# Operand blocks of a late batch prepared one by one, with the sums on VectorE and side work moved

## The chip, the cores and the metric

The kernel runs on one core of a Trainium2 chip. The metric is the device time of one launch in microseconds (us); of the kernel before, the median of three runs is 733.26 us (733.25 to 733.49).

## What is computed

Per batch and head, keys and values are pooled into 32 memory slots by a softmax over the slots, queries attend to those slots, and the result goes through a gated feed-forward layer. Cut to what matters:

```python
a = softmax(phi, axis=slots)                # 8 batches, 8 heads, 576 positions, 32 slots
k_m = einsum('bhsm,bhsd->bhmd', a, k)       # and v_m from v
attn = softmax(q @ k_m.T / 8)               # 576 x 32 per head
x = concat_heads(attn @ v_m)                # 4608 tokens x 512
out = (sigmoid(x @ w_gate) * (x @ w_val)) @ w_out     # 512 -> 1536 -> 512, float32
```

## The kernel before, in words

All engines run hand-written orders: `step` records an operation and chains it behind the last one of every engine it uses, so each engine executes exactly the order in which the program calls `step`.

Batches 0 to 3 and all loads come first (up to about 379 us); the change touches batches 4 to 7, the **late batches**, each some 87 to 89 us long. Such a batch has 12 steps f, one per 128 columns of the hidden layer (`for b, f`, from line 1312). Matrix products are made of three TensorE matmuls each, since every float32 operand is split into a rounded part `hi` (a ScalarE cast) and a rest `lo` (a VectorE subtraction, `rest`, line 179).

The transposed attention of a batch is a 2 x 2 block matrix, b11, b12, b21, b22, each 128 x 288. Seven products take the place of eight: `Group.p(1)` to `p(7)` multiply weight parts with b11, b21, b22 and four sums, t1 = b12 - b11, t2 = b22 - t1, t3 = t2 - b11, t4 = b21 - t2. Product to operand: 1 b11, 2 b21, 3 b22, 4 t4, 5 t1, 6 t2, 7 t3. b12 itself is no operand. Results land in PSUM banks a, b, c, d (one buffer each).

Order of a normal step (b, f), with h the group of the step before: p7 of h, p1, at even f the weights of the next two steps (`pair_u`, 16 small matmuls into banks c and a, copied out by ScalarE as `r_raw` and `l_raw`), one or two output products (`out_tile`: three 128 x 512 matmuls into an accumulator `acc`), p2 (into bank a), p5 (into c), perhaps one output product, p4 of h, p6, an output product, p3, an output product. VectorE adds and multiplies the results (`add`, `product_of`), ScalarE takes sigmoids (`gate`) and casts (`to_hi`, whose rest is `to_lo`); output products of step f run in step f + 2. `part_hi` and `part_lo` split the weights of the next pair, parts r, l and s.

Side work stands at named places of a step ("m", "act", "B", "m2", "end", "Z"), set by a plan per batch (`late_sides`, line 1255). While batch b runs, the plan prepares the attention of batch n = b + 1 (scores, softmax, `normalize`, `cross`, which transposes it into the tile of q, then `sums_at`) and the memory of batch m = b + 2. Loads of q, of the weight ring and the output stores go through SyncE's one queue.

The split operands live in four tiles `at` (128 x 1152 each: hi and lo of the blocks, hi and lo of the sums). There is no room for two batches, so at f = 11 the step **turns** (`turning`): p7 and p4 of the last group are made at once instead of in the next step, and `at_hi`, `at_lo` (lines 936 and 941) split the blocks and then the sums of the next batch, 1152 columns at a time, each behind the last product that reads the old tile. The next batch starts with no group h behind it. The four sums of batches 5 to 7 run on GpSimd (`sums_at(n, nc.gpsimd)`, lines 926 to 934).

Of the kernel before, what the change touches and what calls it, by code (L numbers as in the profile page):

```python
# [13 lines left out]
ALU = mybir.AluOpType  # L14
# [3 lines left out]
P = 128  # L18
B, H, S, D, M = 8, 8, 576, 64, 32
# [79 lines left out]
def attn_moe_kernel(  # L99
# [35 lines left out]
    def att(shape, name, bufs=1):  # L135
        return sb.tile(shape, F32, name=name, bufs=bufs)
# [214 lines left out]

    def a_exp(b):

        ph, nmx = loaded[b, "phi"], loaded.pop((b, "nmx"))
        z = loaded[b, "z"] = att([P, NG], "z")
        for g in range(NG):
# [568 lines left out]

    def sums_at(b, eng):

        (b11, b12, b21, b22), t = [
            [x[:, i * HALF : (i + 1) * HALF] for i in range(4)] for x in raw_at[b]
        ]  # L930
        eng.tensor_tensor(t[0], b12, b11, op=ALU.subtract)
        eng.tensor_tensor(t[1], b22, t[0], op=ALU.subtract)
        eng.tensor_tensor(t[2], t[1], b11, op=ALU.subtract)
        eng.tensor_tensor(t[3], b21, t[1], op=ALU.subtract)

    def at_hi(b, i):

        at.setdefault(b, {})[i] = [at_tile()]
        nc.scalar.copy(at[b][i][0].rearrange("p r n -> p (r n)"), raw_at[b][i])

    def at_lo(b, i):

        at[b][i].append(at_tile())
        hi, lo = [x.rearrange("p r n -> p (r n)") for x in at[b][i]]
        rest(lo, raw_at[b][i], hi)

    def attend(b):
        run(normalize(b))
        yield
        cross(b)  # L950
        sums_at(b, nc.vector)
        yield
# [146 lines left out]
    def side_of(b, name):  # L1099

        i, k = {"b11": (0, 0), "b21": (0, 2), "b22": (0, 3), "t1": (1, 0), "t2": (1, 1), "t3": (1, 2), "t4": (1, 3)}[name]
        return [x.rearrange("p r n -> p (r n)")[:, k * HALF : (k + 1) * HALF] for x in at[b][i]]

# [3 lines left out]
    class Group:  # L1107
# [133 lines left out]
    def out_tile():  # L1241

        if not tiles:
            return
        b, f, t, at_start, at_end = tiles.pop(0)
        hi, lo = [x[:, (t % 2) * P : (t % 2 + 1) * P] for x in G[b, f, t // 2]]
        w_hi, w_lo = wo_of(f)
        if at_start:
            acc[b, t] = po.tile([P, DM], F32, name=f"acc{t}")
        for i, (l, r) in enumerate([(hi, w_hi), (hi, w_lo), (lo, w_hi)]):  # L1250
            matmul(acc[b, t], l, r, start=at_start and i == 0, stop=at_end and i == 2)
        if at_end:
            leave(b, f, t)

    def late_sides(b):
# [11 lines left out]
        if n < B:  # L1267
# [10 lines left out]
            put(7, "act", s_exp, n)  # L1278
            put(8, "B", next, norm)
            put(9, "B", next, norm)  # L1280
            put(10, "B", cross, n)
            put(10, "Z", sums_at, n, nc.gpsimd)
        if m < B:
            def begin_m():
                memories[m] = memory(m)

            put(2, "B", a_max, m)
            put(7, "act", a_exp, m)
            put(7, "Z", a_sum, m)
            put(7, "Z", begin_m)  # L1290
            for f, place in ((8, "m2"), (9, "m"), (10, "m2"), (11, "m")):
                put(f, place, go, m)
                put(f, "end" if place == "m2" else "act", go, m)
            if m + 1 < B:
                put(11, "Z", load_next, m + 1)
        return plan

# [7 lines left out]
    for i in range(2):  # L1305
        step(at_hi, QUAD, i)
        step(at_lo, QUAD, i)
    raw_at.pop(QUAD)
# [3 lines left out]
    for b, f in [(b, f) for b in range(QUAD, B) for f in range(NFT)]:  # L1312
# [7 lines left out]
        n = (b - QUAD) * NP + f // 2  # L1320
        odd, turning = f % 2, f == NFT - 1
        more = n + 1 < NPAIRS
# [10 lines left out]
        if not late_left:  # L1333
            step(next, extra, None)
        wide = (b, f) in LEFT_AT and f != 5 or (f, "m") in plan or not odd and more
        if not odd and more:
# [3 lines left out]
        side("m")  # L1340
        side("m3")
        step(out_tile)
        if wide:
            step(out_tile)
        if h:
            step(h.product_of, 1)
        side("act")
        if not late_left:
# [21 lines left out]
        if h:  # L1370
            step(h.to_hi)
            step(h.to_left)
        if not odd and more:
            step(u_sums, n + 1, 0, 1)
# [5 lines left out]
        side("end")  # L1380
        if turning and b + 1 < B:
            step(at_hi, b + 1, 0)
        if not odd and more:
            step(part_hi, n + 1, "r")
        if odd and more:
            step(part_hi, n + 1, "s")
        step(g.add, 1)
        if late_left:
# [6 lines left out]
        if turning and b + 1 < B:  # L1395
            step(at_lo, b + 1, 0)
        step(g.gate, 0)
        step(g.gate, 1)
        if not odd and more:
            step(u_sums, n + 1, 2)  # L1400
            step(part_hi, n + 1, "l")
# [5 lines left out]
        if f == 0 and b + 1 < B:  # L1407
            load_q(b + 1)
        if h:
            for c in range(2):  # L1410
                put_tiles(h.b, h.f, c, h.f == 0, h.f == NFT - 1)
        if f == 0 and n:
            pairs_of.pop(n - 1)
        if not odd and f:
            pairs_of.pop(n - 1)
        h = g
        if turning:
# [13 lines left out]
            step(out_tile)  # L1431
            h = None
    extra = out_left(B // 2 - 1, 2 * TURN, TURN)
    step(next, extra)
    while tiles:
        step(out_tile)
    step(next, extra)

# [52 lines left out]
```

## Time and profile before

| what | value |
| --- | --- |
| median of three runs | 733.26 us |
| the profiled execution, its own time | 733.32 us |
| its span, first to last instruction | 731.5 us |
| PE busy, share of span | 713.2 us, 97% |
| VectorE (DVE) | 536.3 us, 73% |
| ScalarE (ACT) | 421.0 us, 58% |
| GpSimd (POOL) | 47.5 us, 6% |
| granted TensorE clock, mean | 1.00 |

A busy PE is one with a matmul in it. Since the starts of matmuls of one kind follow at a fixed distance when nothing is late, time lost is read from the distance of two starts. Idle time of the other engines costs nothing by itself.

### The profile page before, as it was taken

The numbers are of one execution on the slowest core, as the hardware profiler recorded it, in microseconds if no ns is written. First come the engines' busy times: TensorE is split into PE (matmuls) and PEld (weight loads), VectorE is DVE, ScalarE is ACT, GpSimd is POOL, SyncE is SP. The second block draws the span as 40 slices with busy tenths as digits, with TensorE's granted clock in tenths as the row PEclk, the third lists the DMA queues.
The fourth block names the chain that finished last, engine by engine and source line by source line (L and its number), as shares of the span: only waits on it lengthen the run. The fifth ranks groups of instructions, "written<-read, shape, count | busy, mean of one in ns | idle before, by whom it ended". The sixth has DMA issues, their size and how long they took to land.

```text
span 731.5 us, 14167 instructions
## 1 busy us (share of the span) xinstructions
PE 713.2 (97%) x5524; PEld 582.4 (80%) x5524; DVE 536.3 (73%) x1021; ACT 421.0 (58%) x969; POOL 47.5 (6%) x83
## 2 busy tenths in 40 slices
PE   8899999999999999999999999999999999999997
PEld 6656778888988988887987788778887887778786
DVE  5999998676877765577458678776787777977663
ACT  4676775464444433245366576765867557676553
POOL 0000100220111110110100002000020000200000
PEclk9999999999999999999999999999999999999999
DMA  8994629659348469861565222643114312141102
GB/s 347 418 386 159 239 87 389 206 162 369 133 159 288 146 194 234 286 225 29 171 274 184 63 110 92 231 150 110 66 59 163 133 58 73 58 173 59 58 1 72
DMA packets 37906, 124.64 MB, mean 170 GB/s; under 512 B 4240, under 2 KB 11664, under 8 KB 31696
## 3 DMA queue, kind: packets, MB, share of 16 engines
q1 hardware_dynamic: 31744, 103.04, 40.1%
q0 software_dynamic: 6096, 20.71, 7.9%
q8 instruction: 43, 0.70, 0.4%
q14 instruction: 23, 0.19, 0.1%
HBM read 94.90 MB, written 28.84 MB: 169 GB/s over the span
## 4 chain that ended last, share of the span: by engine, by line
PE 82%; DVE 11%; ACT 3%; DMA 2%; issue 1%; SPq 0%; DVEq 0%; ACTq 0%
PE acc L189 33%; PE pu_t L189 25%; PE c L189 8%; PE a L189 7%; PE d L189 4%; PE b L189 4%; DMA kvm<-in_kvm_dram 2%; DVE zs L495 1%; DVE at L179 1%; DVE z L1143 1%; DVE z L1150 1%; DVE e L482 1%; DVE e L499 1%; DVE mx L480 1%; DVE e L473 1%
## 5 line engine op out<-in xcount | busy, mean ns | idle before, releaser
L189 PE MATMUL pu_t<-at,u_hi 128*128 128x320 f32 (+1 forms) x752 | 156.2, 303 | 0.2 <-DVE sg L670 0.2
L189 PE MATMUL acc<-wo_hi,g_hi 128*128 128x512 f32 x372 | 151.1, 406 | 0.0
L189 PE MATMUL acc<-wo_hi,g_lo 128*128 128x512 f32 x372 | 147.2, 396 | 1.4 <-DVE g_lo L179 1.4
L189 PE MATMUL acc<-wo_lo,g_hi 128*128 128x512 f32 x372 | 146.5, 394 | 0.0
L189 PEld LDWEIGHTS pu_t<-at,u_hi 128*128 128x128 f32 x752 | 124.2, 188 | 11.8 <-issue 3.0
L189 PE MATMUL pu_t<-at,u_lo 128*128 128x320 f32 (+1 forms) x360 | 106.2, 295 | 0.0
L189 PEld LDWEIGHTS acc<-wo_hi,g_hi 128*128 128x128 f32 x372 | 69.8, 188 | 34.4 <-issue 14.2
L189 PEld LDWEIGHTS acc<-wo_hi,g_lo 128*128 128x128 f32 x372 | 69.8, 188 | 20.1 <-DVE g_lo L179 4.1
L164 ACT ACTIVATE sg<-pu_t 128x256 f32<-128x256 f32 (+1 forms) x94 | 38.7, 411 | 73.2 <-PE pu_t L189 73.0
L189 PEld LDWEIGHTS acc<-wo_lo,g_hi 128*128 128x128 f32 x372 | 70.0, 188 | 6.4
L670 DVE TENSOR_TENSOR sg<-pu_t,sg 128x256 f32<-128x256 f32 (+1 forms) x92 | 41.5, 454 | 39.9 <-ACT sg L164 27.3
L680 ACT CAST g_hi<-sg 128x256 fp32r<-128x256 f32 x90 | 36.4, 406 | 55.8 <-DVE sg L670 54.6
L189 PEld LDWEIGHTS pu_t<-at,u_lo 128*128 128x128 f32 x360 | 67.8, 188 | 0.0
L1139 ACT COPY c_p<-c 128x288 f32<-128x288 f32 x48 | 19.2, 400 | 56.7 <-PE c L189 56.7
L1155 ACT CAST g_hi<-z 128x512 fp32r<-128x512 f32 x48 | 29.8, 621 | 29.7 <-DVE z L1150 29.7
L179 DVE TENSOR_TENSOR g_lo<-sg,g_hi 128x256 fp32r<-128x256 f32 x90 | 37.4, 419 | 11.0 <-ACT g_hi L680 11.0
L1143 DVE TENSOR_TENSOR z<-c,c_x 128x288 f32<-128x288 f32 x48 | 21.8, 454 | 31.3 <-PE c L189 24.6
L1143 DVE TENSOR_TENSOR z<-a,c_s 128x288 f32<-128x288 f32 x48 | 21.9, 456 | 30.2 <-PE a L189 28.9
L164 ACT ACTIVATE z<-z 128x288 f32<-128x288 f32 x96 | 38.2, 438 | 8.5 <-DVE z L1143 8.2
L179 DVE TENSOR_TENSOR u_lo<-pu_t,u_hi 128x512 fp32r<-128x512 f32 (+1 forms) x46 | 28.6, 672 | 10.4 <-ACT u_hi L593 10.4
L179 DVE TENSOR_TENSOR g_lo<-z,g_hi 128x512 fp32r<-128x512 f32 x48 | 33.5, 698 | 3.7 <-ACT g_hi L1155 3.7
L593 ACT CAST u_hi<-pu_t 128x512 fp32r<-128x512 f32 (+1 forms) x46 | 24.0, 587 | 13.8 <-PE pu_t L189 13.7
(252 smaller groups left out, 1480.7 us busy)
## 6 DMA issues: line engine op xcount, KB each, us to landing
ring<-wgv SPq DMA_DIRECT2D x24, 1024.0 KB, 4.8
at<-at SPq DMA_DIRECT2D x24, 576.0 KB, 7.6
kvm<-in_kvm_dram SPq DMA_DIRECT2D x12, 1024.0 KB, 10.1
q<-in_qT_dram SPq DMA_DIRECT2D x16, 512.0 KB, 4.8
part<-row POOLq DMA_DIRECT2D x32, 256.0 KB, 4.8
row<-part SPq DMA_DIRECT2D x32, 256.0 KB, 4.0
wg<-in_kvm_dram SPq DMA_DIRECT2D x4, 1024.0 KB, 11.9
out_dram<-row POOLq DMA_DIRECT2D x16, 256.0 KB, 4.7
```

Of the source, the lines that this page charges most:

```text
L164: last_act[0] = nc.scalar.activation(*args, **kw)
L179: return nc.vector.tensor_tensor(lo, x, hi.bitcast(F32), op=ALU.subtract)
L189: last_pe[0] = do(*args, **kw)
L473: nc.vector.transpose(blocks(b, c)[:, r].rearrange("p w m -> p (w m)"), t)
L480: nc.vector.tensor_reduce(mx, e, axis=AX.X, op=ALU.max)
L482: nc.vector.tensor_tensor(e, e, mx.unsqueeze(3).broadcast_to([P, 2, w, M]), op=ALU.subtract)
L593: nc.scalar.copy(hi[:, r, :nf], U[b, fs[0], "pb"][r])
L670: last_prod[0] = nc.vector.tensor_tensor(prod, ps[1][:, :n], sg[:, :n], op=ALU.mult)
L680: nc.scalar.copy(hi, prod[:, : 2 * P])
L1139: nc.scalar.copy(getattr(self, name), self.c if name == "p5" else self.d)
L1143: nc.vector.tensor_tensor(self.z[:, i], x, y, op=ALU.add)
L1155: nc.scalar.copy(self.g[0], self.z[:, 2:4, : 2 * P])
```

## The change

1. The four `at` tiles become eight **rooms** of 288 columns (hi and lo). Seven hold the operands of the running batch, one is spare. When the last product that reads a room has been issued (f = 11, or f = 0 of the next batch for products 7 and 4), its room goes to the next free block of the next batch. `at_hi` and `at_lo` handle one block, in the order b11 (f = 10), b21, t1, t2 (f = 11), b22, t3, t4 (f = 0 of the next batch).
2. The turn goes: p7 and p4 of the last group run in the next batch's step 0, as in any other step, except in the very last step.
3. The four sums run on VectorE, two at f = 10 and two at f = 11.
4. Side work moves: `normalize` from places B of f = 8 and 9 to E and Z of f = 8, `cross` from f = 10 to the end of f = 9; the exponentials of `a_exp` are set apart; the cast of part l moves from the end of an even step to the start of the odd one, behind its first copy; the copies of the memory move with it; the copies of finished accumulators (`leave`) wait for `leave_late`; the load of the next batch's q stands behind the split of t4.

```diff
-    def at_hi(b, i):
...
-        at.setdefault(b, {})[i] = [at_tile()]
-        nc.scalar.copy(at[b][i][0].rearrange("p r n -> p (r n)"), raw_at[b][i])
...
+    def at_hi(b, name):
+        k = room_of_at[b, name] = free_rooms.pop(0)
+        nc.scalar.copy(at_rooms[k][0], raw_of(b, name))
+
+    def at_lo(b, name):
+        hi, lo = at_rooms[room_of_at[b, name]]
+        rest(lo, raw_of(b, name), hi)
...
             self.product(getattr(self, where), x, t, start)
+            if self.f == NFT - 1:
+                free_rooms.append(room_of_at.pop((self.b, t)))
...
-            put(8, "B", next, norm)
-            put(9, "B", next, norm)
-            put(10, "B", cross, n)
-            put(10, "Z", sums_at, n, nc.gpsimd)
+            put(8, "E", next, norm)
+            put(8, "Z", next, norm)
+            put(9, "Z", cross, n)
+            put(10, "B", sums_at, n, 1, 2)
+            put(10, "act2", at_hi, n, "b11")
+            put(10, "Z", at_lo, n, "b11")
+            put(11, "m", at_hi, n, "b21")
+            put(11, "E", sums_at, n, 3, 4)
+            put(11, "B", at_lo, n, "b21")
+            put(11, "act2", at_hi, n, "t1")
+            put(11, "B2", at_lo, n, "t1")
+            put(11, "act3", at_hi, n, "t2")
+            put(11, "Z", at_lo, n, "t2")
+        if b > QUAD:
+            put(0, "act", at_hi, b, "b22")
+            put(0, "act", at_hi, b, "t3")
+            put(0, "E", at_lo, b, "b22")
+            put(0, "B", at_lo, b, "t3")
+            put(0, "act2", at_hi, b, "t4")
+            put(0, "B2", at_lo, b, "t4")
...
-            put(7, "act", a_exp, m)
+            put(7, "act1", a_exp, m, (0,))
+            put(7, "act2", a_exp, m, (1,))
...
-                put(f, "end" if place == "m2" else "act", go, m)
+                put(f, "end" if place == "m2" else "m", go, m)
...
         side("m3")
+        if odd and more:
+            step(part_hi, n + 1, "l")
         step(out_tile)
...
-        if turning and b + 1 < B:
-            step(at_hi, b + 1, 0)
...
-        if turning:
+        last = b == B - 1 and f == NFT - 1
+        if last:
             step(g.p, 7)
             step(g.add, 3)
...
-        if f > 1:
+        if f > 1 or b > QUAD:
             step(out_tile)
...
-            if b + 1 < B:
-                step(at_hi, b + 1, 1)
-                step(at_lo, b + 1, 1)
-                raw_at.pop(b + 1)
...
-            h = None
```

Three places show how the engines' orders move (names: `at` split operands, `q` the raw blocks, `z` the group's results, `g_hi`/`g_lo` their split, `c_s`, `c_p`, `c_x` copies of banks, `r_raw`, `l_raw`, `s_raw` raw weights, `u_`/`s_` their splits).

ScalarE from step 11 of batch 6 into step 0 of batch 7, before and then with the change:

```order
L939 CAST at<-q 128x1152
L1085 CAST s_hi<-s_raw 128x768
L164 ACTIVATE z<-z 128x288 x2
L939 CAST at<-q 128x1152
L1155 CAST g_hi<-z 128x512
L1165 COPY left<-z 128x64
L1139 COPY c_s_7628<-d 128x288
L1067 COPY r_raw<-a 128x512
```

```order
L1171 CAST g_hi<-z 128x512
L1181 COPY left<-z 128x64
L957 CAST at<-q 128x288
L1101 CAST s_hi<-s_raw 128x768
L164 ACTIVATE z<-z 128x288 x2
L957 CAST at<-q 128x288
L1155 COPY c_s_7620<-d 128x288
L1083 COPY r_raw<-a 128x512
L1083 COPY l_raw<-c 128x512
L957 CAST at<-q 128x288 x2
```

The second cast of the last group (`g_hi`, `left`) no longer stands between the casts of `at` and the copy `r_raw`; two casts of 288 columns do, and more follow behind `l_raw`.

VectorE in step 10 of batch 6, from the results of step 9 to the rest `g_lo`, before and then with the change:

```order
L1143 TENSOR_TENSOR z<-b,c_p_7396 128x288
L1150 TENSOR_TENSOR z<-z 128x288
L1143 TENSOR_TENSOR z<-a,c_s_7456 128x288
L924 STREAM_TRANSPOSE q<-e 128x1152
L1150 TENSOR_TENSOR z<-b,z 128x288
L1082 TENSOR_TENSOR s_raw<-r_raw,l_raw 128x256
L1082 TENSOR_TENSOR s_raw<-s_raw,l_raw 128x256
L1143 TENSOR_TENSOR z<-c,c_x 128x288
L179 TENSOR_TENSOR g_lo<-z,g_hi 128x512
```

```order
L926 STREAM_TRANSPOSE q<-e 128x1152
L1159 TENSOR_TENSOR z<-b,c_p_7408 128x288
L1166 TENSOR_TENSOR z<-z 128x288
L1159 TENSOR_TENSOR z<-a,c_s_7470 128x288
L932 TENSOR_TENSOR q<-q 128x288 x2
L1166 TENSOR_TENSOR z<-b,z 128x288
L1098 TENSOR_TENSOR s_raw<-r_raw,l_raw 128x256
L1098 TENSOR_TENSOR s_raw<-s_raw,l_raw 128x256
L1159 TENSOR_TENSOR z<-c,c_x 128x288
L179 TENSOR_TENSOR g_lo<-z,g_hi 128x512
```

The transpose (`cross`) goes ahead of the step's three first operations, and two of the four sums (L932) come in where it stood.

ScalarE in steps 8 and 9 of batch 4, before and then with the change (`row<-a` copies the transposed weights of the memory out of bank a):

```order
L388 COPY row<-a 128x512
L1085 CAST u_hi<-r_raw 128x512
L164 ACTIVATE z<-z 128x288 x2
L1085 CAST u_hi<-l_raw 128x512
L1139 COPY c_s_5323<-b 128x288
L388 COPY row<-a 128x512
```

```order
L390 COPY row<-a 128x512
L1101 CAST u_hi<-r_raw 128x512
L164 ACTIVATE z<-z 128x288 x2
L1155 COPY c_s_5323<-b 128x288
L390 COPY row<-a 128x512
L1101 CAST u_hi<-l_raw 128x512
```

The cast of part l now stands behind the second copy out of bank a instead of ahead of it.

## Rows read from the trace of the kernel before

**Rows 1.** Batch 5: its length; busy PE, PEld, DVE, ACT, POOL; PE clock; DMA
```profile
468.62:557.60 88.98, 87.40 (x673) 70.53 (x674) 67.97 (x130) 60.11 (x138) 3.76 (x4) 1.00 0.29 100
```

**Rows 2.** Waits of PE, 380 to 732 us: for whom, us in total, times, longest
```profile
PE a L189 <- ACT r_raw L1067: 3.5, 3, 1.3
PE acc L189 <- DVE g_lo L179: 1.4, 2, 1.1
PE a L189 <- ACT row L388: 0.9, 2, 0.4
```

**Rows 3.** Timeline of PE at the turn from batch 4 to 5: start, us, what
```profile
462.25 0.39 PE L189 MATMUL acc<-wo_hi,g_hi 128*128 128x512 f32 x1
462.48 0.40 PE L189 MATMUL acc<-wo_lo,g_hi 128*128 128x512 f32 x1
462.90 0.50 PE L189 MATMUL acc<-wo_hi,g_lo 128*128 128x512 f32 x1
463.24 0.43 PE L189 MATMUL b<-at,u_hi 128*128 128x288 f32 x2
...
463.64 0.39 PE L189 MATMUL acc<-wo_hi,g_hi 128*128 128x512 f32 x1
...
464.83 0.61 PE L189 MATMUL c<-ring,vT 64*32 64x512 f32 x1
...
465.85 0.50 PE L189 MATMUL acc<-wo_hi,g_hi 128*128 128x512 f32 x1
...
467.12 0.39 PE L189 MATMUL acc<-wo_hi,g_lo 128*128 128x512 f32 x1
468.62 0.53 PE L189 MATMUL a<-at,s_hi 128*128 128x288 f32 x2 [1.12 <-ACT r_raw L1067]
```

**Rows 4.** Timeline of ScalarE at the same turn
```profile
463.75 1.16 ACT L939 CAST at<-q 128x1152 fp32r<-128x1152 f32 x1
467.02 0.62 ACT L1155 CAST g_hi<-z 128x512 fp32r<-128x512 f32 x1 [2.12 <-DVE z L1150]
...
467.69 0.39 ACT L1139 COPY c_s<-d 128x288 f32<-128x288 f32 x1
467.98 0.59 ACT L1067 COPY r_raw<-a 128x512 f32<-128x512 f32 x1
```

**Rows 5.** Timeline of VectorE at the same turn
```profile
465.27 1.35 DVE L179 TENSOR_TENSOR at<-q,at 128x1152 fp32r<-128x1152 f32 x1
466.54 0.45 DVE L1150 TENSOR_TENSOR z<-b,z 128x288 f32<-128x288 f32 x1
467.67 0.69 DVE L179 TENSOR_TENSOR g_lo<-z,g_hi 128x512 fp32r<-128x512 f32 x1 [0.69 <-ACT g_hi L1155]
```

**Rows 6.** Timeline of ScalarE, steps 8 and 9 of batch 4
```profile
441.92 0.61 ACT L1085 CAST u_hi<-l_raw 128x512 fp32r<-128x512 f32 x1
...
442.72 0.59 ACT L388 COPY row<-a 128x512 f32<-128x512 f32 x1
```

**Rows 7.** Timeline of VectorE, step 10 of batch 6
```profile
628.05 1.37 DVE L924 STREAM_TRANSPOSE q<-e 128x1152 f32<-128x1152 f32 x1
...
629.68 1.04 DVE L1082 TENSOR_TENSOR s_raw<-r_raw,l_raw 128x256 f32<-128x256 f32 x1
...
631.97 0.91 DVE L179 TENSOR_TENSOR g_lo<-z,g_hi 128x512 fp32r<-128x512 f32 x1
```

**Rows 8.** Timeline of PE, start of step 11 of batch 6
```profile
631.41 0.40 PE L189 MATMUL acc<-wo_lo,g_hi 128*128 128x512 f32 x1
632.94 0.50 PE L189 MATMUL acc<-wo_hi,g_lo 128*128 128x512 f32 x1 [1.14 <-DVE g_lo L179]
```

**Rows 9.** The first of the four sums: ns min/median/max, first and last start us
```profile
L931 POOL TENSOR_TENSOR q<-q x3: 804/809/811, 452.9 to 629.6; 128x288 f32<-128x288 f32 x3
L931 DVE TENSOR_TENSOR q<-q x1: 459/459/459, 337.1 to 337.1; 128x288 f32<-128x288 f32 x1
```

**Rows 10.** DMA issues of the page: KB each, median us from issue to landing
```profile
q<-in_qT_dram SPq DMA_DIRECT2D x16, 512.0 KB, 4.8
```

More of the change, by code (lines that the diff above doesn't have):

```diff
@@ L350, in a_max, with a_exp @@
         loaded[b, "nmx"] = nmx
[L352 to L356, printed above, removed]
+    def a_exp(b, gs=range(NG)):
+        ph, nmx = loaded[b, "phi"], loaded[b, "nmx"]
+        if 0 in gs:
+            loaded[b, "z"] = att([P, NG], "z")
+        z = loaded[b, "z"]
+        for g in gs:
             curve(
@@ L924, in cross, with sums_at, raw_of, first_hi @@
         nc.vector.transpose(raw_at[b][0], loaded[b, "e"])
[L926 to L934, printed above, removed]
-    def at_hi(b, i):
-        at.setdefault(b, {})[i] = [at_tile()]
-        nc.scalar.copy(at[b][i][0].rearrange("p r n -> p (r n)"), raw_at[b][i])
[L941 to L945, printed above, removed]
+    def sums_at(b, *which):
+        for i in which:
+            x, y = [("b12", "b11"), ("b22", "t1"), ("t2", "b11"), ("b21", "t2")][i - 1]
+            nc.vector.tensor_tensor(raw_of(b, f"t{i}"), raw_of(b, x), raw_of(b, y), op=ALU.subtract)
+    ROOMS = {"b11": 0, "b12": 1, "b21": 2, "b22": 3, "t1": 4, "t2": 5, "t3": 6, "t4": 7}
+    at_rooms, free_rooms, room_of_at = [], [], {}
+    def raw_of(b, name):
+        i, k = divmod(ROOMS[name], 4)
+        return raw_at[b][i][:, k * HALF : (k + 1) * HALF]
+    def first_hi(b, i):
+        if i == 0:
+            whole = [[at_tile() for _ in range(2)] for _ in range(2)]
+            whole = [[x.rearrange("p r n -> p (r n)") for x in part] for part in whole]
+            at_rooms.extend([x[:, k * HALF : (k + 1) * HALF] for x in part] for part in whole for k in range(4))
+            room_of_at.update({(b, name): k for name, k in ROOMS.items() if name != "b12"})
+            free_rooms.append(ROOMS["b12"])
+            at[b] = whole
+        nc.scalar.copy(at[b][i][0], raw_at[b][i])
+    def first_lo(b, i):
+        rest(at[b][i][1], raw_at[b][i], at[b][i][0])
+    def at_hi(b, name):
[4 more added lines that the diff above has]
+        rest(lo, raw_of(b, name), hi)
     def attend(b):
@@ L950, in attend @@
         cross(b)
-        sums_at(b, nc.vector)
+        sums_at(b, 1, 2, 3, 4)
         yield
@@ L1099, in side_of @@
     def side_of(b, name):
-        i, k = {"b11": (0, 0), "b21": (0, 2), "b22": (0, 3), "t1": (1, 0), "t2": (1, 1), "t3": (1, 2), "t4": (1, 3)}[name]
-        return [x.rearrange("p r n -> p (r n)")[:, k * HALF : (k + 1) * HALF] for x in at[b][i]]
+        return at_rooms[room_of_at[b, name]]
     def late_bank(name):
@@ L1252, in out_tile, with leave_late @@
         if at_end:
-            leave(b, f, t)
+            leaving.append((b, f, t))
+    leaving = []
+    def leave_late():
+        while leaving:
+            leave(*leaving.pop(0))
     def late_sides(b):
@@ L1292, in late_sides @@
                 put(f, place, go, m)
-                put(f, "end" if place == "m2" else "act", go, m)
+                put(f, "end" if place == "m2" else "m", go, m)
             if m + 1 < B:
                 put(11, "Z", load_next, m + 1)
+        if b + 1 < B:
+            put(0, "load", load_q, b + 1)
         return plan
@@ L1305, in attn_moe_kernel @@
     for i in range(2):
-        step(at_hi, QUAD, i)
-        step(at_lo, QUAD, i)
+        step(first_hi, QUAD, i)
+        step(first_lo, QUAD, i)
     raw_at.pop(QUAD)
@@ L1320, in attn_moe_kernel @@
         n = (b - QUAD) * NP + f // 2
-        odd, turning = f % 2, f == NFT - 1
+        odd = f % 2
         more = n + 1 < NPAIRS
@@ L1334, in attn_moe_kernel @@
             step(next, extra, None)
-        wide = (b, f) in LEFT_AT and f != 5 or (f, "m") in plan or not odd and more
+        wide = (b, f) in LEFT_AT and f != 5 or (f, "m") in plan and (f != NFT - 1 or b + 2 < B) or not odd and more
         if not odd and more:
@@ L1346, in attn_moe_kernel @@
             step(h.product_of, 1)
+        step(leave_late)
         side("act")
@@ L1353, in attn_moe_kernel @@
             step(part_lo, n + 1, "r")
+        side("E")
         step(g.add, 0)
         step(g.copy, "p5")
+        side("act1")
         if odd and more:
@@ L1372, in attn_moe_kernel @@
             step(h.to_left)
+        side("act2")
         if not odd and more:
@@ L1387, in attn_moe_kernel @@
         step(g.add, 1)
+        step(leave_late)
         if late_left:
             step(next, extra, None)
-        if turning:
+        last = b == B - 1 and f == NFT - 1
+        if last:
             step(g.p, 7)
@@ L1394, in attn_moe_kernel @@
             step(h.to_lo)
-        if turning and b + 1 < B:
-            step(at_lo, b + 1, 0)
+        side("B2")
         step(g.gate, 0)
         step(g.gate, 1)
+        side("act3")
         if not odd and more:
             step(u_sums, n + 1, 2)
-            step(part_hi, n + 1, "l")
         if odd and more:
             step(part_lo, n + 1, "s")
-        if f > 1:
+        if f > 1 or b > QUAD:
             step(out_tile)
         side("Z")
-        if f == 0 and b + 1 < B:
-            load_q(b + 1)
+        side("load")
         if h:
@@ L1411, in attn_moe_kernel @@
                 put_tiles(h.b, h.f, c, h.f == 0, h.f == NFT - 1)
[L1412 to L1415, printed above, removed]
+        if (f == 0 or not odd) and n:
+            pairs_of.pop(n - 1, None)
         h = g
-        if turning:
+        if last:
             step(out_tile)
@@ L1436, in attn_moe_kernel @@
         step(out_tile)
+        step(leave_late)
     step(next, extra)
```

## The prediction

> **What bounds the kernel now.** First the busy time by stretch: in batch 5 PE has a matmul in it for 87.40 of 88.98 us, DVE for 67.97, ACT for 60.11 [rows 1]. PE sets the time; a gain must come out of the 1.58 us in which it stands still, and work moved between DVE, ACT and POOL counts only where PE waits for it. [...] Next the waits of PE over the late batches: three for `r_raw`, 3.5 us in all, two for `g_lo`, 1.4, two for the memory's copy `row`, 0.9 [rows 2]. Last the timelines, to see what each stall costs and what stood ahead of its releaser.
>
> **A stall costs more than its idle time.** Matmuls of an output product start 0.23 us apart (462.25, 462.48). At the turn the third starts 0.42 after the second: 0.19 lost, though no idle time is listed. The next start then comes 0.34 later instead of 0.23, 0.11 more to refill [rows 3]. Later PE starts its last output matmul at 467.12 and the next product at 468.62: 1.50 instead of 0.23, 1.27 lost for 1.12 listed [rows 3]. So I add 0.15 and a refill of 0.11 to each listed wait.
>
> **Why PE waits at the turn.** Product 2 of the new batch needs bank a, which holds raw weights until ACT's copy `r_raw` at 467.98, 0.59 long, has ended, at 468.57 [rows 4]; PE had filled the bank soon after its last weight matmuls, so before 465.85 [rows 3]. ACT came late because it first waited 2.12 us for the old group's result, cast it (`g_hi`, 467.02) and copied `c_s` [rows 4]. That result (DVE, 466.54) stood behind the second split of `at`, 1.35 long from 465.27 [rows 5]. So the chain is: split of 1152 columns, result, cast, copy, PE.
>
> **Removed.**
> - The three `r_raw` waits: 3.5 + 3 x (0.15 + 0.11) = 4.3.
> - The short `g_lo` stall ahead of each turn, where products 7 and the added `add` crowd in: 3 x (0.19 + 0.11) = 0.9, taking the other two turns for like the first.
> - The `row` waits at step 9 (batches 4 and 5): 0.9 + 2 x 0.26 = 1.4. Product 2 waits there for the copy of 442.72; ahead of it stands the cast of part l, start 441.92, 0.61 long [rows 6]. The cast goes behind the copy, which takes more off than the 0.45 that each of the two waits lists, so they end. Who then waits for the later cast: `part_lo` l, on DVE, behind the first result of step 9; its product is in step 10, so nobody on PE.
> - The `g_lo` waits of batch 6: 1.4 + 2 x 0.26 = 1.9. The large one is 632.94 after 631.41, 1.53 instead of 0.23 [rows 8]. On DVE `cross` (1.37) stood in step 10 ahead of the chain to `g_lo`, and the weight sums behind it took 1.04, `g_lo` 0.91 against 0.69 at the turn [rows 5, 7] while POOL made its sums from 629.6 on [rows 9]. Now `cross` is at the end of step 9 and POOL is still. The small one, at step 9, stood behind `normalize`; it moves into the idle time of DVE ahead of the first result of step 8.
>
> Sum of what can go: 4.3 + 0.9 + 1.4 + 1.9 = 8.5.
>
> **Added.** Per turn DVE gets four sums of 0.46 [rows 9], 1.84. The early batches ran one there at that price. Eight splits of 288 columns take the place of two of 1152. No row has them: DVE's nearest is the 288-column result, 0.45 [rows 5], so 3.6 against 2.7; bounds 0.34 (a quarter of 1.35) and 0.69 (512 columns) [rows 5]. I take 0.45, the same size and engine. On ACT eight casts at 0.39, by the copy of the same size [rows 4] (bounds 0.29, a quarter of 1.16, and 0.61 [rows 6]), 3.1 against 2.3. DVE gains about 2.7 busy us, ACT 0.8; DVE gets back what POOL's sums cost it, 0.6 for one weight sum alone if it takes the 0.4 of a 288-column operation. In batch 5 that makes DVE about 70 of 89, so it does not bound a batch; the question is the three steps at a turn.
>
> **The turn counted through.** I took the new orders of the four engines from step 8 to step 1, each operation behind its engine's last and behind what it reads, with the durations above, 0.08 of overlap between neighbours (465.27 to 466.54 is 1.27 for an operation of 1.35 [rows 5]), products at 0.40 (463.24 to 463.64) and output products at 0.70 [rows 3]. Steps 10 and 0 last 6.7 us on PE (seven products, four output products, 1.0 for raw weights, 464.83 to 465.85 [rows 3]), step 11 lasts 5.6, in batches 4 and 5 some 2.3 more for memory matmuls. The tightest turn is 6 to 7, without them. There, from product 7 of step 11 on: DVE works on step 11's list from 1.2 to 8.3, that is 2.7 us into step 0; `product_of(0)` of group 10 is done at 5.1, before product 1 of the new step, which writes its bank, at 6.0. ACT follows it: cast 5.6, t1, part s, two sigmoids, t2, `c_s`, then `r_raw`, done at about 8.7. Product 2 can start at 8.9. The blocks are ready in time: b11 at 1.2 for 6.0, b21 at 4.7 for 8.9, t1 at 6.8 for 9.3, t2 at 8.3 for 10.1, b22 at 10.0 for 11.2, t3 at 10.7 for 12.3, t4 at 13.3 for 15.3. At the other two turns everything has 1 to 2 us more. Step 10 of batch 6 ends `g_lo` 0.8 before its need. So I expect no stall of size; I allow 0.4 for the 0.2 of room at the tightest place.
>
> **Moved past queues.** The q load on SP now waits for the split of t4 (about 13.3, near the end of step 0), with only output stores and weight-ring loads behind it. Its first use is step 3, some 18 us from the start of step 0; two loads of 4.8 us [rows 10] and a smaller one end before it even one after the other. Later accumulator copies on ACT free `acc` one step ahead of reuse. GpSimd's queue only loses work. PE keeps all its matmuls. Cost zero; were q late by 5 us, scores would stall PE for that in two batches.
>
> The sum, against the profiled execution of 733.3 (span 731.5; it is 0.06 from the median): 733.3 - 8.5 + 0.4 = **725.2 us**.
>
> **The rivals.**
> - *The wait survives at the turn.* ACT still casts t1 and t2 and part s ahead of `r_raw`, behind the result of group 10, which DVE gives only after sums, splits and weight rests. If DVE is a microsecond later than I count, product 2 waits as before. If each turn keeps 1.3 us, 3.9 comes back: 729.1. For: room of 0.2 at turn 6 to 7. Against: 1 to 2 us at the others.
> - *Slower: DVE bounds the turn.* Over steps 10, 11 and 0 DVE has at full durations 15 results (6.8), five rests of 512 columns (3.5), one of 768 (about 1.0) and six weight sums (some 0.4 each, 2.4), 13.7 us, and 5.4 of splits and sums: 19.1, against 19.0 for PE at the last turn. If no overlap holds and each block waits for ACT's cast and delays the results behind it, PE waits for lo parts and bank releases one after another. It decides from 3.3 us of new wait per turn (9.9 against 8.5); at 3.5 the time is 735.3. Against: the 0.08 overlaps and the 21 us at the other turns. [...]
> - *No change:* the stall shifts to another wait at the turn and the other gains are eaten: about 733.
>
> **How the numbers follow.** The forecast, 723.8 to 727.3, has 0.60; the surviving wait, up to 731.8, 0.22; no change 0.07; slower 0.11. The low end is 8.5 whole and one us of losses too short for the list of waits, as the 0.19 above was. The dear bounds, 0.69 for a split and 0.61 for a cast, add 3.7 us to a turn's two engines; most of it falls on spare time at two turns and makes the surviving wait at the third. The range reaches to 730.0, through most of that rival. A measurement can tell 0.2%, 1.5 us, from no change: faster 0.82, same 0.07, slower 0.11.
>
> **What would show it.** Right: no PE wait over 0.3 us for `r_raw`, `row` or `g_lo` in batches 4 to 6, steps 11 and 0 without a gap, 288-column splits near 0.45, `s_raw` sums at 0.4 everywhere. Wrong: PE waits for `at` parts, for `r_raw` in step 0, or for q in step 3; a DVE without idle time from step 10 to step 0.

## The result and the profile after

The changed kernel takes **725.81 us** (median of four runs, 725.69 to 727.13) against 733.36 for the kernel before beside it: a ratio of 0.990, 95% interval 0.988 to 0.992. Forecast: 725.2, range 723.8 to 730.0.

| what | before | after |
| --- | --- | --- |
| span of the profiled execution, us | 731.5 | 723.9 |
| PE busy, share of span | 713.2, 97% | 710.5, 98% |
| VectorE busy | 536.3, 73% | 535.6, 74% |
| ScalarE busy | 421.0, 58% | 423.0, 58% |
| GpSimd busy | 47.5 | 36.3 |

Batch 5, cut at product 2 of step 0 as in [rows 1]: length, then busy PE, PEld, DVE, ACT, POOL, PE clock, DMA share and GB/s.

```profile
464.85:552.00 87.15, 86.52 (x675) 70.85 (x674) 67.71 (x139) 60.70 (x143) 0.00 (x0) 1.00 0.31 103
```

PE now stands still for 0.63 us there instead of 1.58, and VectorE is no busier. Of the list of waits of PE over the late batches one line is left, for a wait in step 8, where there was none before ([rows 2] shows three of the list's four lines; the fourth, a wait of 0.3 us for VectorE, is shown below under "Late copies of accumulators"):

```profile
PE a L189 <- ACT r_raw L1083: 1.2, 2, 0.6
```

At the turn from batch 4 to 5, PE's timeline (start, us, what) goes from the last output product of the old group into product 2 of the new batch without a gap, where [rows 3] lost 1.27 us:

```profile
464.39 0.39 PE L189 MATMUL acc<-wo_lo,g_hi 128*128 128x512 f32 x1
464.61 0.40 PE L189 MATMUL acc<-wo_hi,g_lo 128*128 128x512 f32 x1
464.85 0.43 PE L189 MATMUL a<-at,s_hi 128*128 128x288 f32 x2
```

ScalarE there, to be read beside [rows 4]: the cast `g_hi` of the group before starts 1.8 us ahead of the first weight matmul (462.32), and `r_raw` starts at 463.58, so it is out at 464.17, 0.68 us ahead of product 2.

```profile
460.55 0.62 ACT L1171 CAST g_hi<-z 128x512 fp32r<-128x512 f32 x1 [0.31 <-DVE z L1166]
...
462.97 0.42 ACT L957 CAST at<-q 128x288 fp32r<-128x288 f32 x1
463.29 0.39 ACT L1155 COPY c_s<-d 128x288 f32<-128x288 f32 x1
463.58 0.59 ACT L1083 COPY r_raw<-a 128x512 f32<-128x512 f32 x1
```

At the tightest turn, 6 to 7, a little of the wait is left, and the trace shows it only in the starts: product 2 begins 0.42 after the last output matmul instead of 0.23. First PE, then ScalarE:

```profile
634.43 0.39 PE L189 MATMUL acc<-wo_hi,g_lo 128*128 128x512 f32 x1
634.85 0.53 PE L189 MATMUL a<-at,s_hi 128*128 128x288 f32 x2
```

```profile
631.19 0.62 ACT L1171 CAST g_hi<-z 128x512 fp32r<-128x512 f32 x1 [1.13 <-DVE z L1166]
...
634.22 0.58 ACT L1083 COPY r_raw<-a 128x512 f32<-128x512 f32 x1
```

Sizes, from the costliest groups after 375 us (count, busy us and mean ns, idle time of the engine just before):

```profile
L179 DVE TENSOR_TENSOR at<-q,at 128x288 fp32r<-128x288 f32 x21 | 9.5, 453 | 0.9 <-ACT at L957 0.8
L932 DVE TENSOR_TENSOR q<-q 128x288 f32<-128x288 f32 x12 | 5.2, 453 | 0.1
L957 ACT CAST at<-q 128x288 fp32r<-128x288 f32 x21 | 8.7, 433 | 0.0
L1098 DVE TENSOR_TENSOR s_raw<-r_raw,l_raw 128x256 f32<-128x256 f32 x23 | 9.6, 415 | 0.0
```

**Where the time went, by pairs of steps.** Each even step starts its 16 weight matmuls with the same instruction (`c<-ring,vT`; 464.83 in [rows 3], 462.32 after). The distance of one such start to the next covers two steps and doesn't depend on what happened earlier. In us, for the pairs that differ most (columns by step; b is the batch; the two turn columns hold steps 10 and 11, the columns behind them steps 0 and 1 of the next batch):

| kernel | b4 0-1 | b4 6-7 | b4 8-9 | turn 4-5 | b5 0-1 | b6 8-9 | turn 6-7 | b7 0-1 |
| --- | --- | --- | --- | --- | --- | --- | --- | --- |
| before | 11.10 | 15.45 | 14.13 | 17.07 | 12.48 | 13.19 | 15.97 | 12.25 |
| after | 10.57 | 15.22 | 14.24 | 14.98 | 12.83 | 12.39 | 12.36 | 12.78 |
| e4, turn kept | 11.10 | 15.21 | 14.25 | 17.07 | 12.49 | 12.39 | 14.43 | 12.25 |
| e7, rests twice | 10.58 | 15.21 | 14.25 | 14.98 | 13.09 | 12.39 | 13.01 | 13.77 |
| e1, exp in one | 10.58 | 15.45 | 13.41 | 14.98 | 12.83 | 12.39 | 12.36 | 12.79 |
| e2b, first exp early | 10.57 | 15.22 | 13.96 | 14.98 | 12.83 | 12.39 | 12.36 | 12.78 |
| e9, exp around c_p | 10.57 | 15.22 | 13.65 | 14.98 | 12.83 | 12.39 | 12.36 | 12.77 |
| e5, cast back | 10.57 | 15.21 | 14.25 | 14.98 | 12.83 | 12.39 | 12.36 | 12.78 |
| e12, only the cast | 11.10 | 15.45 | 13.61 | 17.08 | 12.47 | 13.18 | 15.97 | 12.27 |
| e6, cross back | 10.57 | 15.21 | 14.44 | 15.98 | 12.83 | 12.98 | 13.39 | 13.09 |
| e3, sums on GpSimd | 10.57 | 15.21 | 14.23 | 14.98 | 12.83 | 12.39 | 12.37 | 12.39 |
| e10, e9 and e3 | 10.57 | 15.21 | 13.66 | 14.98 | 12.83 | 12.39 | 12.37 | 12.39 |
| e11, leave at once | 11.10 | 15.22 | 14.24 | 14.98 | 12.83 | 12.39 | 12.36 | 12.77 |

A turn and the pair behind it belong together, since p7 and p4 moved from one to the other. Batch 5 repeats columns 2 to 5 within 0.05. Two smaller differences have no column: steps 2-3 of batch 4 take 13.16 before and 13.35 after, and steps 2-3 of the batch behind each turn lose some 0.4 in e7.

### The profile page after: what moved, and what is told of

Its sections match the earlier page's. It is cut to its first block, busy times and chain, and to the rows that moved or that the text cites. A ratio compares the mean times of both kernels' runs of the same rounds, so it can differ in the third digit from the quotient of the medians.

```text
span 723.9 us, 14181 instructions
## 1 busy us (share of the span) xinstructions
PE 710.5 (98%) x5524; PEld 583.4 (81%) x5524; DVE 535.6 (74%) x1048; ACT 423.0 (58%) x984; POOL 36.3 (5%) x71
## 4 chain that ended last, share of the span: by engine, by line
PE 87%; DVE 6%; ACT 3%; DMA 2%; issue 1%; SPq 0%; DVEq 0%; ACTq 0%
PE acc L189 36%; PE pu_t L189 25%; PE c L189 8%; PE a L189 8%; PE b L189 5%; PE d L189 5%; DMA kvm<-in_kvm_dram 2%; ACT ph L164 1%; DVE e L484 1%; DVE e L501 1%; DVE zs L497 1%; DVE mx L482 1%; DVE e L475 1%; DMA q<-in_qT_dram 0%; SPq L175 0%
```

## The experiments

Theory: the turn's gain comes from the rooms alone (parts 1 and 2 of the change), the rest from side work on VectorE and ScalarE, and the new wait in step 8 from the exponential. Rivals: the sums' engine or the casts carry it. Medians and ratios to the kernel before on the same chip:

| kernel | median us (runs) | ratio, 95% interval |
| --- | --- | --- |
| e4 | 730.64 (4) | 0.9963, 0.9950 to 0.9976 |
| e7 | 728.87 (4) | 0.9939, 0.9924 to 0.9954 |
| e1 | 724.86 (4) | 0.9885, 0.9870 to 0.9899 |
| e2b | 725.27 (4) | 0.9889, 0.9874 to 0.9904 |
| e2 | 725.09 (4) | 0.9887, 0.9872 to 0.9902 |
| e9 | 724.43 (4) | 0.9880, 0.9867 to 0.9894 |
| e5 | 725.85 (4) | 0.9900, 0.9883 to 0.9916 |
| e12 | 732.41 (11) | 0.9988, 0.9979 to 0.9997 |
| e6 | 729.98 (4) | 0.9953, 0.9937 to 0.9970 |
| e3 | 725.23 (4) | 0.9890, 0.9875 to 0.9904 |
| e10 | 724.25 (4) | 0.9877, 0.9863 to 0.9890 |
| e11 | 726.02 (4) | 0.9900, 0.9885 to 0.9915 |

### The turn

**e4** is the kernel before with parts 3 and 4 of the change (but for the late copies of accumulators and the place of the q load), its turn kept:

```diff
-            put(8, "B", next, norm)
-            put(9, "B", next, norm)
-            put(10, "B", cross, n)
-            put(10, "Z", sums_at, n, nc.gpsimd)
+            put(8, "E", next, norm)
+            put(8, "Z", next, norm)
+            put(9, "Z", cross, n)
+            put(10, "B", sums_at, n, 1, 2)
+            put(11, "E", sums_at, n, 3, 4)
...
+        if odd and more:
+            step(part_hi, n + 1, "l")
```

> The kernel before with only the sums on VectorE and the side work at its new places; the turn stays, blocks are split 1152 columns at a time. Theory: the waits for row (1.4) and g_lo in batch 6 (1.9) go, the step 8 waits of the change (2.0) come and the step 7 stalls (0.5) go, the turn's 5.2 stay: 733.3 - 1.4 - 1.9 - 0.5 + 2.0 = 731.5, between 730.5 and 732.5. Rival: the turn is worth little and the moved side work brought the gain: under 728. Or the turn alone brought all of it: 733 or more.

730.64. In the table the turn and the pair behind it cost 29.56 with the old turn and 27.81 with rooms, at 6 to 7 26.68 and 25.14: the rooms are worth 1.75 twice and 1.54, 5.0 in all. The three waits of the turns are still in e4's list, beside the two new ones of step 8:

```profile
PE a L189 <- ACT r_raw L1068: 4.8, 5, 1.3
```

The rooms bring two things at once, pieces of 288 columns and the products 7 and 4 put off into the next batch, and no run has one without the other. In the changed kernel the cast `g_hi` that stands ahead of `r_raw` at the turn 6 to 7 is that of group 10 (631.19); that of the last group starts at 637.25, behind `r_raw`. So the order alone takes the old group's result and cast out of the copy's way, and what the small pieces add to it is not shown.

**e7** makes every block's rest twice, which adds some 3.2 us of VectorE work to each turn (seven blocks of 0.45) and changes no result:

```diff
         rest(lo, raw_of(b, name), hi)
+        rest(lo, raw_of(b, name), hi)
```

> The change with every rest of a block made twice (the same result written again), 8 x 0.45 = 3.6 us more on DVE at each turn. Theory: the turns 4 to 5 and 5 to 6 have 1 to 2 us of room and lose under 1 each; the turn 6 to 7 has 0.2 and loses 1 to 2, for r_raw in step 0 or g_lo: 727 to 729. Rival, DVE already bounds the turns: every turn loses some 3, over 733. Rival, room everywhere: under 726.3.

728.87, so 9.5 us of work cost 3.1 by the medians and 3.5 by the pairs. At the turn 4 to 5 PE loses nothing in steps 10 and 11, 0.26 in steps 0 and 1 and 0.4 later; at 6 to 7 it loses 0.65, 0.99 and 0.4. VectorE has room at two turns and next to none at the third.

### The new wait in step 8

In the changed kernel ScalarE runs the exponentials of step 7 (`ph`) behind the copy `c_p`; its timeline in batch 4:

```profile
428.24 1.17 ACT L164 ACTIVATE e<-e 128x1152 f32<-128x1152 f32 x1
429.89 0.40 ACT L1155 COPY c_p<-c 128x288 f32<-128x288 f32 x1 [0.48 <-PE c L189]
430.18 0.78 ACT L164 ACTIVATE ph<-ph,nmx 128x576 f32<-128x576 f32 x1
...
431.90 0.78 ACT L164 ACTIVATE ph<-ph,nmx 128x576 f32<-128x576 f32 x1
...
433.51 1.28 ACT L164 ACT_TABLE_LOAD   x1
434.81 0.78 ACT L164 ACTIVATE z<-z 128x288 f32<-128x288 f32 x2
...
435.77 0.59 ACT L1083 COPY r_raw<-a 128x512 f32<-128x512 f32 x1
```

And PE:

```profile
435.40 0.40 PE L189 MATMUL acc<-wo_hi,g_lo 128*128 128x512 f32 x1
436.41 0.54 PE L189 MATMUL a<-at,s_hi 128*128 128x288 f32 x2 [0.62 <-ACT r_raw L1083]
```

ScalarE idles 0.48 us ahead of `c_p`, and the return of the sigmoid's table (1.28) and `r_raw` run 0.3 us later than in the kernel before (table load at 433.21 there), while PE, which no longer waits for `c_p` and has won 0.3 earlier in the batch, asks 0.5 earlier (the output matmul starts at 435.40, before at 435.91): 1.01 instead of 0.23 between the two starts.

**e1** puts both pieces back ahead of `c_p`:

```diff
-            put(7, "act1", a_exp, m, (0,))
-            put(7, "act2", a_exp, m, (1,))
+            put(7, "act", a_exp, m)
```

> The change with the exponentials of a_exp put back behind s_exp in one piece. Theory: the two waits of PE for r_raw in step 8 (batches 4 and 5, 0.6 listed each, 0.8 lost with 0.2 to refill) are there because ACT now stands idle 0.5 us ahead of its copy of bank c in step 7 and reloads its sigmoid table that much later; with the exponentials in one piece these waits go and a stall of some 0.25 per batch for bank c in step 7 comes back: 725.8 - 2 x 0.7 = 724.4. Rival: PE merely asks earlier for the copy, since nothing holds it up in step 7 any more, and the order of the exponentials is worth nothing: 725.6 to 726.0.

724.86, between theory and rival. By pairs: steps 8-9 win 0.83, steps 6-7 lose 0.23, since `c_p` is late again. So the split of the exponential costs 1.2 net over two batches.

**e2b** puts only the first piece ahead of `c_p`; **e2** also takes `r_raw` ahead of `c_s`:

```diff
-            put(7, "act1", a_exp, m, (0,))
+            put(7, "act", a_exp, m, (0,))
             put(7, "act2", a_exp, m, (1,))
...
-        step(g.copy, "s1")
+        if odd or not more:
+            step(g.copy, "s1")
...
             step(u_out, n + 1, "r")
+            step(g.copy, "s1")
             step(u_out, n + 1, "l")
```

(the first hunk is e2b, all of it e2)

> The change with the first group's exponential right behind s_exp, ahead of the copy of bank c in step 7, the second where the change has it. Theory: ACT's idle 0.5 us in step 7 is filled, the table is reloaded 0.5 earlier, the waits in step 8 shrink from 0.8 to 0.3 each, and bank c is copied in time: 725.8 - 2 x 0.5 = 724.8, to 724.4 if the refill goes too. Rival: the copy of bank c becomes late and the time stays: 725.6 to 726.2.

> As the run with the first exponential early, and in even steps ACT copies r_raw ahead of c_s, so bank a is free 0.3 earlier everywhere. Theory: nothing of the step 8 waits is left, and the 0.2 (0.3 with the refill) for r_raw at the turn 6 to 7 goes as well: 725.8 - 2.0 - 0.3 = 723.5. Rival: c_s late by 0.6 makes the first result of even steps late on DVE, and what follows it costs more than it gives: 725 to 727.

725.27 and 725.09: e2b lies between its theory and its rival, e2 misses its theory and lies in its rival's range, though not for the rival's reason, since no pair is longer than in e2b by more than 0.01. Steps 8-9 are at 13.96 and 13.97: a second piece at the old late place keeps ScalarE late, and with `r_raw` first the next product waits 0.28 for `l_raw` instead, in step 8 and at the turn 6 to 7 alike. Order among the copies is not the matter; how soon ScalarE is through with them is.

**e9** puts the pieces on both sides of `c_p`:

```diff
-            put(7, "act1", a_exp, m, (0,))
-            put(7, "act2", a_exp, m, (1,))
+            put(7, "act", a_exp, m, (0,))
+            put(7, "act1", a_exp, m, (1,))
```

> The changed kernel with the two pieces of the last exponential put around the copy of c_p in step 7: the first ahead of it, the second right behind it. Theory: the waits of step 8 for r_raw (0.78 and 0.79 us in batches 4 and 5) come from ScalarE standing idle ahead of c_p and making a piece of the exponential later; here the idle time is filled, c_p is not late either, so both go and nothing takes their place: 725.8 - 2 x 0.83 = 724.1 us (723.8 to 724.5). Rival: c_p is late as it was with the exponential in one piece, and some 0.2 us per batch come back in step 7: 724.4 to 724.9. Other rival: ScalarE is busy without a gap from there to r_raw, the waits of step 8 shrink only: 725.0 to 725.6.

724.43. Its ScalarE has no idle time in that stretch, `c_p` is not late for PE, and the table load comes 0.6 earlier than in the changed kernel (0.7 by the clock of the traces, of which 0.1 lies ahead of batch 4):

```profile
429.20 0.77 ACT L164 ACTIVATE ph<-ph,nmx 128x576 f32<-128x576 f32 x1
...
429.95 0.38 ACT L1155 COPY c_p<-c 128x288 f32<-128x288 f32 x1
430.24 0.78 ACT L164 ACTIVATE ph<-ph,nmx 128x576 f32<-128x576 f32 x1
...
432.81 1.28 ACT L164 ACT_TABLE_LOAD   x1
```

Both batches win 0.59 in steps 8-9 and give nothing back. The time is in the theory's range, but by its pairs the kernel wins 1.2 and not 1.66: 0.2 us of the wait is left in each batch, as the last rival said, with ScalarE now busy throughout.

### The row waits of step 9

**e5** takes the cast of part l back to the end of the even step:

```diff
-        if odd and more:
-            step(part_hi, n + 1, "l")
         step(out_tile)
...
             step(u_sums, n + 1, 2)
+            step(part_hi, n + 1, "l")
```

> The change with the cast of part l back at the end of the even step, ahead of the next step's copies. Theory: in step 9 of batches 4 and 5 the memory's copy out of bank a is 0.6 later again and PE waits for it, 0.7 with the refill each, and step 1 of batch 4 loses some 0.3: 725.8 + 1.7 = 727.5, between 727.0 and 728.0. Rival: the copies' new place m took the wait away and the cast is worth nothing: 725.6 to 726.0.

725.85, nothing lost: the rival's time, but not its reason. The copy `row` stands behind the cast of part l again, as in [rows 6], and is out at 442.47, 0.47 ahead of product 2:

```profile
441.07 0.61 ACT L1101 CAST u_hi<-l_raw 128x512 fp32r<-128x512 f32 x1
...
441.87 0.60 ACT L390 COPY row<-a 128x512 f32<-128x512 f32 x1
```

```profile
442.94 0.42 PE L189 MATMUL a<-at,s_hi 128*128 128x288 f32 x2
```

What made it early is the normalising, which has left its old place on VectorE: ScalarE's `g_hi` ahead of `row` starts at 438.55 instead of 439.56 (in e6, with the normalising back, it waits 1.07 us for VectorE, as in the kernel before, and in e5 it waits for nothing). PE also comes later, by the 0.8 that it loses in step 8; whether the earlier normalising would be enough without that loss is not shown.

**e12** does the reverse, the kernel before with that cast alone moved (the edit of e4's last two lines, and the copies of the memory from "act" to "m"):

> The kernel before with only the cast of part l (and the copies of the memory beside it) at the places of the change; turns, sums, normalising and all else as before. Theory: this alone takes the waits of step 9 for ScalarE's row copies away, since either of the two moves does: 733.3 - 1.4 = 731.9 us (731.5 to 732.4). Rival: only the normalising moved a step earlier does it, and the time stays 733.3 within 0.3.

732.41, at the edge of the theory's range: steps 8-9 win 0.52 in batch 4 and 0.54 in batch 5, and no wait for `row` is listed. A short one is left: product 2 starts 0.30 after the last output matmul instead of 0.23, and the refill costs 0.11 more.

```profile
443.25 0.40 PE L189 MATMUL acc<-wo_hi,g_lo 128*128 128x512 f32 x1
443.55 0.53 PE L189 MATMUL a<-at,s_hi 128*128 128x288 f32 x2
```

So the cast alone takes 1.06 us of the two waits, and the theory that either move does all of it is half shown: the cast is not quite enough, and the earlier normalising was enough in the changed kernel, with PE held up in step 8.

**e6** takes normalising and `cross` back to their places, everything else as changed:

```diff
-            put(8, "E", next, norm)
-            put(8, "Z", next, norm)
-            put(9, "Z", cross, n)
+            put(8, "B", next, norm)
+            put(9, "B", next, norm)
+            put(10, "B", cross, n)
             put(10, "B", sums_at, n, 1, 2)
```

> The change with normalize at places B of steps 8 and 9 and the transpose at place B of step 10 again, ahead of the first two sums. Theory: in step 10 DVE's chain to g_lo is 1.37 later against 0.8 of room, so batch 6 waits 0.6 to 0.9 at the start of step 11, and 0.5 for g_lo at step 9; batches 4 and 5 have their memory matmuls as cover: 726.5 to 727.5. Rival, that GpSimd's sums and not the transpose made g_lo late: no wait comes back, 725.5 to 726.0.

729.98: both missed by some 2.5 us and more. In batch 6 the theory's places hold, 0.59 lost in steps 8-9 and 1.03 at the turn; what it missed is 1.0 at each of the other two turns, by a wait that nobody had named. The list of PE's waits, then ScalarE and PE in step 10 of batch 4:

```profile
PE a L189 <- ACT tails L397: 1.8, 2, 0.9
PE a L189 <- ACT r_raw L1083: 1.6, 3, 0.6
PE acc L189 <- DVE g_lo L179: 0.7, 2, 0.4
```

```profile
453.94 0.62 ACT L1171 CAST g_hi<-z 128x512 fp32r<-128x512 f32 x1 [1.60 <-DVE z L1166]
...
454.94 0.53 ACT L397 COPY tails<-a 64x128 f32<-64x128 f32 x2
```

```profile
455.52 1.08 PE L189 MATMUL a<-kvm,row 128*32 128x128 f32 x32 [0.90 <-ACT tails L397]
```

With `cross` (1.37) and two sums ahead of the group's result on VectorE, ScalarE gets the result late, and behind its cast stand b11's cast and the copies `tails`, for which the memory matmuls wait. Those matmuls were my spare time of turns 4 to 5 and 5 to 6; they have a need of their own.

### The sums

**e3** gives the four sums of batches 5 to 7 back to GpSimd, at the places of the change:

```diff
-            nc.vector.tensor_tensor(raw_of(b, f"t{i}"), raw_of(b, x), raw_of(b, y), op=ALU.subtract)
+            (nc.gpsimd if b > QUAD else nc.vector).tensor_tensor(raw_of(b, f"t{i}"), raw_of(b, x), raw_of(b, y), op=ALU.subtract)
```

> The change with the four sums of batches 5 to 7 on GpSimd, at the same places. Theory: no engine but DVE gains or loses, and DVE is not waited for at the turns: 1.84 us of sums leave it and its weight sums and rests beside GpSimd take up to twice as long, so the time stays within 0.6 us, 725.4 to 726.4. Rival, that the sums on VectorE are a source of the gain: t1 and t2 come late and g_lo is slowed as before, PE waits again for g_lo or for blocks, 727 to 729.

725.23: faster by 0.6, below the range of the theory. By pairs it wins 0.39 behind the turn 6 to 7 and nothing anywhere else: the last of the wait for `r_raw` is gone there. GpSimd makes the sums in 3.81 us; while it does, three of VectorE's operations take longer (step 10 of batch 6 in e3):

```profile
622.63 0.89 DVE L1166 TENSOR_TENSOR z<-z 128x288 f32<-128x288 f32 x1
...
624.62 0.92 DVE L1098 TENSOR_TENSOR s_raw<-s_raw,l_raw 128x256 f32<-128x256 f32 x1
...
625.83 0.93 DVE L179 TENSOR_TENSOR g_lo<-z,g_hi 128x512 fp32r<-128x512 f32 x1
```

The same three in the changed kernel:

```profile
622.67 0.46 DVE L1166 TENSOR_TENSOR z<-z 128x288 f32<-128x288 f32 x1
...
625.08 0.43 DVE L1098 TENSOR_TENSOR s_raw<-s_raw,l_raw 128x256 f32<-128x256 f32 x1
625.79 0.68 DVE L179 TENSOR_TENSOR g_lo<-z,g_hi 128x512 fp32r<-128x512 f32 x1
```

They lose 0.43, 0.49 and 0.25, 1.17 in all, all in step 10, where there is time for it; the 0.82 of the last two sums is saved in step 11, where there is none. The three have both inputs in SBUF and started while GpSimd worked on its sums (622.41 to 626.22); results that read a PSUM bank kept their 0.44 to 0.45 among them. Both inputs in SBUF are not enough, though: the weight sum at 624.18 has them too and kept its 0.41. It started at about the end of GpSimd's second sum, by an estimate of 0.95 for each of the four in 3.81; whether that is the reason is not shown.

**e10** is e9 and e3 together:

> The same with the four sums of batches 5 to 7 on GpSimd at the places of the changed kernel. Theory: VectorE is the engine that TensorE waits for at the turn from batch 6 to batch 7 and nowhere else, so this takes another 0.4 us there (as it did alone) and the two gains add: 723.7 us (723.3 to 724.2). Rival: the gain of the sums was a matter of single executions, and this is equal to the kernel with the exponential alone moved, within 0.1 us.

724.25, the best median of all (single runs from 723.86) and 0.05 above the theory's range. The pairs add as expected, another 0.38 behind the turn 6 to 7. The medians of e9 and e10 alone, 0.18 apart with overlapping intervals, don't tell them apart; the opening, below, moves single executions by more.

### Late copies of accumulators

**e11** makes them at once, as before:

```diff
         if at_end:
-            leaving.append((b, f, t))
+            leave(b, f, t)
```

> The changed kernel with the leaving of a raw tile made in its old place at once, not put off behind the other VectorE work of the step. Theory: putting it off is what took the wait of 0.46 us for VectorE's z in the first two steps of batch 4 away (the two steps took 11.10 us before and 10.57 after); here the two steps take 11.0 to 11.1 again and the kernel 726.3 us (726.0 to 726.6). Rival: another part of the change took it, and the time stays 725.8 within 0.2.

726.02, the low end of the theory. The first pair of batch 4 takes 11.10 again, and PE waits where the kernel before waited, for VectorE's result in bank c. First the line of the list of before that [rows 2] leaves out, then e11:

```profile
PE c L189 <- DVE z L1143: 0.3, 1, 0.3
```

```profile
388.50 0.61 PE L189 MATMUL c<-ring,vT 64*32 64x512 f32 x1 [0.30 <-DVE z L1159]
```

VectorE adds a finished accumulator to `row` (0.68 us) ahead of that result:

```profile
387.41 0.68 DVE L732 TENSOR_TENSOR row<-acc,row 128x512 f32<-128x512 f32 x1
388.00 0.44 DVE L1159 TENSOR_TENSOR z<-c,c_x 128x288 f32<-128x288 f32 x1
```

The theory's place is shown; the size is smaller than expected, because the next pair gives 0.19 back (13.35 becomes 13.16): 0.34 net.

## Why the prediction was right

The forecast was 0.6 under the median and the mechanism holds. That it came so near is in part luck: the working left out a cost of 1.2, and the gains came out 0.9 larger than it had them, 0.3 of that from a move to which it gave no gain. By its steps:

- **The turn**: forecast 4.3 for `r_raw`, 0.9 for the short stalls, less 0.4; 4.8 net. Measured 5.0 (e4), of which the three waits are gone at two turns and nearly so at the third. The rival "the wait survives" is out at 4 to 5 and 5 to 6; at 6 to 7 it survives with 0.2.
- **The turn counted through.** Product 7 of step 11 starts at 625.68 and `r_raw` ends at 634.80: 9.1, where I counted 8.7; product 2 could have started at 9.0. So the room of 0.2 was in truth -0.1, and the 0.4 allowed for it is what e3 gives back: 0.39.
- **The `g_lo` waits of batch 6**: forecast 1.9. Measured 0.80 in steps 8-9 and 1.54 at the turn (e4 against before), 2.3. GpSimd's interference was not the cause by itself: in e3 it slows the same chain in step 10 and no wait comes back. With normalising, `cross` and two sums back ahead of that chain 0.59 and 1.03 come back (e6); how the rest divides is not shown.
- **The `row` waits**: forecast 1.4, and 1.40 is what steps 8-9 win when the exponential is out of the way (14.13 to 13.41 in e1, 0.68 in batch 5). In batch 4's pair the starts on PE differ between e1 and the kernel before at product 2 of step 9 alone. The reason given, the cast, is worth 1.06 of the 1.40 by itself (e12), and was not needed in the changed kernel (e5).
- **What the working left out.** It gave no cost to the split of `a_exp`, one of the changes in the list, though it could be worked out from the trace of before: in step 7 of batch 4 the exponential of `e` ends at 429.70 and the product that fills bank c at 430.09, so ScalarE stands idle if `c_p` comes next, and the table load behind the exponentials comes later by that. It cost 1.2 net. Nor did it give a gain to the late copies, since [rows 2] left out the wait that they take away: 0.34 (e11). "No PE wait over 0.3 us for `r_raw`" was wrong for this step 8.
- **VectorE's price.** A split is 453 ns, as taken (0.45), a cast 433 and not 390, a weight sum 415 as taken. I counted eight splits and casts per turn; seven are made (21 over three turns), since b12 is no operand. VectorE is no busier than before, where I had it at 70 us in batch 5 (67.7 measured): the 69 weight sums of the late batches fell from a mean of 0.49 to 0.42, 5.1 us in all, and I had counted that gain for one sum. The rival "VectorE bounds the turn" is near the truth at one turn of three: from step 10 to step 0 VectorE is busy for 18.1 of 19.6 us at 6 to 7 (18.3 of 22.2 at 4 to 5), and e7 pays 2.0 us of its 3.5 there. In the changed kernel it cost the 0.4 that e3 gives back. Four splits of 288 columns take 1.81 us of VectorE against 1.35 in one, and the kernel is faster all the same, since `r_raw` no longer stands behind a split, a result and a cast of the old group.
- **Covers**: the q load was issued at 469.69 and first used at 481.92, its three pieces took at most 4.8 us each to land, and no wait for q is listed. The memory matmuls as spare time were a wrong cover (e6); here it cost nothing, because `cross` had moved.

Sum of the pairs: -5.0 (turns), -2.3 (`g_lo`), -1.4 (`row`), +1.2 (exponential), -0.3 (late copies), and +0.2 of small differences with the tail and the opening, -7.6: the spans differ by 731.5 - 723.9.

## What to carry to other kernels

A preparation that needs the old data's buffer can be cut into as many pieces as the buffer has last readers; what is won is not the preparation's own time (VectorE pays more for it, 1.81 us in four pieces against 1.35 in one) but the time that short, urgent operations of the same engines no longer stand behind it. When stalls are taken out of the bounding engine, list every operation that the change shifts, also the ones that look harmless, and ask of each who asks earlier now; here one exponential took back 1.2 of 9.0. Give work to the engine that is late nowhere at that place: GpSimd, slower with 0.80 to 1.00 us a sum (e3) against 0.45 to 0.46, was the better home for the sums, because the 1.17 us that it cost VectorE at the turn 6 to 7 fell into a step with room.

## What the hardware showed unexpectedly

In some executions the granted TensorE clock fell to about half in the opening, after 27.4 us: over the 3.6 us from there it was 0.53 in the profiled executions of e1, e10 and e12, and 1.00 in those of the kernel before and the changed kernel. One row each for the stretches from 20 and 27.4 us (length, busy engines, clock), first the changed kernel, then e10:

```profile
20.00:27.40 7.40, 4.93 (x133) 3.08 (x137) 7.12 (x15) 3.04 (x8) 0.00 (x0) 1.00 1.03 428
27.40:31.00 3.60, 3.60 (x59) 3.18 (x52) 3.34 (x8) 2.37 (x6) 0.00 (x0) 1.00 1.00 408
```

```profile
20.00:27.40 7.40, 4.78 (x125) 2.86 (x125) 7.12 (x15) 3.08 (x8) 0.00 (x0) 1.00 1.02 423
27.40:31.00 3.60, 3.31 (x46) 2.54 (x47) 3.34 (x8) 1.62 (x4) 0.00 (x0) 0.53 1.00 411
```

PE had been busy for 4.8 to 4.9 of the 7.4 us before in both; in the changed kernel 2.4 us of that stretch are waits for the load of `wg`. The first sum of batch 4 on VectorE then starts at 337.9 in e10 instead of 337.2 in the changed kernel and 337.1 in e3, both of the same program up to there, so it costs up to 0.8 us, as much as some of the experiments above differ by; the table of pairs is free of it, the medians are not. Why one execution falls and another doesn't stays open.
